# Zero-weight fillers, another gate for the last chunk's MLP weights, and a re-planned order in a fused attention and MLP block

## The chip, the core and the metric

The kernel runs on one core of one Trainium2 chip. The time is the device time of one execution in microseconds (us); what is compared is the median over runs. Five engines work side by side, each through its own instruction queue: TensorE (PE, matmuls; its weight loads are shown apart as PEld), VectorE (DVE), ScalarE (ACT), GpSimd (POOL) and SyncE (SP). Nearly all DMA transfers are issued by SP, one after the other.

## The reference, cut to what matters

```python
x = A_x                                   # 1 x 2048 x 640, bf16
mod = (silu(c) @ w_mod).reshape(1, 6, 1, 640)
sa, ca, ga, sb, cb, gb = mod[:, 0] ... mod[:, 5]
h = layernorm(x) * (1 + ca) + sa
q, k, v = split(h @ wqkv)                 # 32 heads of 20
p = softmax(q @ k.T * 20 ** -0.5)         # 2048 x 2048 for each head
x = x + ga * ((p @ v) @ wo)
h = layernorm(x) * (1 + cb) + sb
x = x + gb * (((h @ w_gate) * (h @ w_up)) @ w_down)   # 640 -> 1536 -> 640
```

The 32 score matrices of 2048 x 2048, their exponentials and their products with V are most of the work.

## The kernel before, in words

**Chunks and items.** The queries are cut into six chunks (L474): 512, 512, 256, 256, 256 and 256 of them. In each chunk there are eight items, each a set of four heads. An item walks over the 2048 keys in 16 key tiles of 128. In one group, PE multiplies four heads at a time by matmuls that each use 32 rows of the array (L1511, `ps_all<-QT,KT`), into a pair of PSUM banks. There are two such pairs for ACT, so that PE fills one while ACT works on the other.

**Exponentials.** Most groups go to ACT: one activation of 128 x 1024 (L1548) writes bf16 probabilities to `PP`. The rest is done by DVE with integer arithmetic on the bits of the number, in "D units": L1572 (scores to int16 bits, `DB`), L1604 and L1612 (two masks, `DSS`), and a product of the two by DVE (L1609) or POOL (L1624).

**Products with V.** `PP` or `DSS` times `Vf` (L2177) go into the running bank of the item: a PSUM bank in which each item sums over its key tiles, in four quadrants of 32 rows. `Vf` holds V of every head with a column of ones (for the sum of the softmax), and behind the last head a column block of zeros. The item's end is T1 (L1704), a reciprocal (L1709), the normalisation T3 (L1711, POOL) and T4 (L1720), and then four or five small DMAs on SP into `Ocp` (L1732).

**Suffix of a chunk.** Once a chunk's items are done, `suffix(ci)` does the output projection, the second layernorm, its transpose `h2T`, twelve rounds of gate and up (L961, `ps_all<-h2T,stg`), their product `hprod`, the down projection (L961, `ps_all<-wd,hprod`) and the output. For the chunks before the last, this work is spread between the scores of the next chunk. Its gate and up weights come in pairs of 160 KB each (L1917, SP) into a ring of three buffers, `stg`; a pair is asked for once its buffer is free. The last chunk's suffix has nothing to hide behind. Ten of its twelve pairs have buffers of their own, `stx`, and in the kernel before they may be asked for as soon as chunk 4's attention output has been written out.

**Start.** Q, K and V are computed from x in the first 270 us, just ahead of the items that need them. Q and K go through rows in DRAM: `q_rows` and `k_rows` are written and then loaded in another layout as `QT` (L1289) and `KT`. Unused rows of `q_rows` are zeroed by DMAs that each cover 512 tokens (L1441, `q_rows<-Ocp`, 393 KB).

**The planner.** Nothing in the loops above fixes the order of instructions. A planner in Python (`Sched`, driven by `pick_pe` and its helpers) runs before compilation: it steps through time with a cost for each task (constants such as `PE_SWITCH` for PE going from one kind of matmul to another, `PV_W` for a product pass, `HAM_*` and `FILL_*` for keeping PE busy) and writes out a fixed order for PE, ACT, DVE, POOL and SP. `emit_program` adds the semaphores. A task has a priority and a gate, which is the number of score groups before which it is not taken. `STAGE` overrides constants item by item. Its numbers shape the order; on the chip, each instruction simply starts when its engine comes to it and its semaphores are there.

**Fillers.** Where the planner thinks that PE would fall idle too long, `do_fill` puts in matmuls whose result nobody reads: identity times a broadcast identity, into a free general bank (L2510), four quadrants of 512 columns.

Of the kernel before, what the change touches and what calls it, by code (L numbers as in the profile page):

```python
# [12 lines left out]

SEM = 60.0
PE_DRAIN = 170.0
PE_SWITCH = 102.0
PE_BACK = 112.0
PV_W = 219.0
X_FIRST = 0.0
ACT_LAT = 250.0  # L20
DVE_LAT = 40.0
# [10 lines left out]
STEAL_END = 66197.894  # L32
STEAL_GAP = 200
HAM_W = 3413.3
HAM_MIN = 2550.0
LKTOL = 300.0


# [92 lines left out]
class Sched:  # L131
# [143 lines left out]
    def step_engine(self, eng):  # L275
        if self.free_at[eng] > self.t:
            return False
        self.pull(eng)
        rl = self.readyl[eng]
        for k, task in enumerate(rl):  # L280
            if task.dead:
                self.readyl[eng] = rl = [x for x in rl if not x.dead]
                return self.step_engine(eng)
            if task.gate > self.progress or (task.cond is not None and not task.cond()):
                continue
            if self.locked(eng, task):
                continue
            if self.acquire(task, self.t):
                rl.pop(k)
                self.lock(eng, task)  # L290
                self.finish_issue(task, self.t, task.dur)
                self.free_at[eng] = self.t + task.dur
                return True
        if eng == "act":
            return self.steal()
        return False
# [53 lines left out]
def emit_program(nc, sched, nsem_dma=56):  # L350
# [130 lines left out]
PV_KEEP = 2  # L481
# [10 lines left out]
EAGER = 7  # L492
# [3 lines left out]
XBACK = 0  # L496
HOLD = 110
PVTOL = 249
XDPRIO = 1.343
# [2 lines left out]
GU_ONE = 1  # L502
XCONT = 0
T3_POOL = 1
HEAD_OUT = 2
NPS = 4
TS_4X, TT_2X = 600.0, 1145.0
# [21 lines left out]
PREEMPT = 0.0  # L529
PRE_M = 0.3  # L530
PV0N = 1
GATE_F = (0.446, 0.6, 0.5, 0.5, 0.5, 1.0)
FILL_MIN = 4190.746
FILL_HARD = 3000.0
FILL_T0, FILL_TH, FILL_MINH = 2300.0, 17000.0, 7500.0
FILL_MODE = 'P'
DUP_MIN = 0.0
# [17 lines left out]
NTERM = 2  # L555

STAGE = {
    0: {"D_LATE": 16, "PVMIN": 2, "X_LATE": -179.96, "XDPRIO": 1.343, "LKTOL": 300.0, "FILL_MIN": 4190.746, "HOLD": 95, "TPRIO": 0.75, "PVTOL": 249, "EAGER": 9, "X_HALF": 0.0, "XBACK": 0, "D_RES": 74, "PVCAP": 12, "PVMAX": 14, "STEAL_GAP": 200, "PV_KEEP": 2},
    2: {"DL": 0.376},
    4: {"HOLD": 53.4},  # L560
    5: {"HOLD": 88.7, "STEAL_GAP": 176.5},
    7: {"DL": 0.501},
    9: {"LKTOL": 115.1},
    10: {"X_HALF": 5.8},
    11: {"DL": 0.443, "EAGER": 4, "FILL_MIN": 3731.3, "X_HALF": 38.6},
    12: {"DL": 0.459, "LKTOL": 438.4, "STEAL_GAP": 303.4, "EAGER": 10, "X_HALF": 21.8},
    13: {"DL": 0.417, "FILL_MIN": 4496.3, "STEAL_GAP": 266.2, "X_HALF": 20.9},
    15: {"LKTOL": 166.0, "PVMAX": 5, "EAGER": 10, "XBACK": 1},
    16: {"PVCAP": 10, "PVMAX": 3, "EAGER": 10, "FILL_MIN": 5086.4},
    17: {"X_HALF": -35.2},  # L570
    18: {"EAGER": 3, "X_LATE": -36.1, "HOLD": 42.4, "PVMIN": 1},
    19: {"DL": 0.471, "EAGER": 2, "X_HALF": 94.7},
    20: {"DL": 0.391},
    21: {"EAGER": 6, "FILL_MIN": 4510.3, "X_HALF": 24.2, "D_LATE": 5},
    22: {"PVMAX": 7, "X_HALF": 147.8, "EAGER": 9, "X_LATE": -21.9, "HOLD": 66.8},
    23: {"HOLD": 124.7, "X_HALF": 14.5},
    24: {"DL": 0.464},
    25: {"DL": 0.549, "PV_KEEP": 3, "X_LATE": 36.2},
    26: {"DL": 0.411, "X_LATE": 65.8, "PVMAX": 3, "EAGER": 8},
    27: {"DL": 0.473, "XBACK": 1, "HOLD": 186.0, "FILL_MIN": 3881.8, "X_LATE": -1.8},  # L580
    28: {"X_HALF": 33.6, "FILL_MIN": 4310.0, "XBACK": 0},
    29: {"PVMAX": 7, "X_LATE": -9.2},
    30: {"X_LATE": -109.9, "HOLD": 140.4, "XBACK": 1},
    31: {"X_LATE": 202.7, "D_RES": 21},
    32: {"PVCAP": 11, "X_HALF": -25.7, "X_LATE": 197.5},
    33: {"DL": 0.442},
    34: {"PVMIN": 5, "X_HALF": 27.8, "XBACK": 1},
    35: {"X_HALF": -31.6, "PVMAX": 14},
    36: {"DL": 0.524},
    37: {"X_LATE": -50.4},  # L590
    40: {"XBACK": 1, "HOLD": 36.3},
    41: {"X_LATE": 52.1, "X_HALF": -52.1},
    44: {"X_LATE": -66.5, "EAGER": 4, "D_RES": 10},
    47: {"FILL_MIN": 5302.0},
    48: {"PVCAP": 14, "FILL_MIN": 3192.3},
}
XHALF = 1
STG_G0, STG_G, XC_G = 12, -10, -20
# [12 lines left out]
def build_kernel(nc, A_x, A_wqkv, A_wo, B_x, B_w_gate, B_w_up, B_w_down, c, w_mod, out):  # L611
# [195 lines left out]
    def dve(dur, f, deps=(), prio=3.0, **k):  # L807
        return sc.add(Task("dve", dur, f, deps, prio=prio, **k))
# [770 lines left out]
    for qi, (it, us) in enumerate(dquads):  # L1579
# [36 lines left out]
        if X_POOL and qi % X_POOL == X_POOL - 1 and qi < len(dquads) - X_LAST and all(  # L1616
                dquads[z][0] == it for z in range(qi, min(len(dquads), qi + X_TAIL + 1))):
            st_["xby"] = None
            for x in range(X_PIECES):
                w = 2048 // X_PIECES  # L1620

                def fxp(e, x=x, w=w, st_=st_):
                    d = DSl[st_["ss"][0]][:, x * w:x * w + w].bitcast(BF16)
                    return e.tensor_tensor(d, DBl[st_["slot"]][:, x * w:x * w + w].bitcast(BF16), d, ALU.mult)  # L1624
                t = Task("pool", w * POOL_NS + 180.0, fxp, [tm, te], prio=2.0 + .1 * qi + .01 * x, name=f"XP.{qi}")
                t.lk = 2
                t.cond = lambda st_=st_: st_["xby"] != "dve"

                def on_p(task, x=x, st_=st_):
                    if x == 0:  # L1630
                        st_["xby"] = "pool"
                        st_["xd"].dead = True
                        sc.left -= 1
                    xjob[0] = X_PIECES - 1 - x
                    if x == X_PIECES - 1:
                        sB0.done(st_["slot"], task)
                        st_["src"][0] = [task]
                t.on_start = on_p
                sc.add(t)
                st_.setdefault("xps", []).append(t)  # L1640
            t = term(fx, [tm, te], TT_2X, "X", src=0, last=True)
            st_["xd"] = t
            t.prio = XDPRIO + .001 * qi
            c0, o0 = t.cond, t.on_start
            t.cond = lambda c0=c0, st_=st_: st_["xby"] is None and c0() and xjob[0] >= XBACK

            def on_x(task, o0=o0, st_=st_):
                o0(task)
                st_["xby"] = "dve"
                for x in st_["xps"]:  # L1650
                    x.dead = True
                sc.left -= X_PIECES
                sc.nx += 1
            t.on_start = on_x
        else:
            term(fx, [tm], TT_2X, "X", src=0, last=True)
# [37 lines left out]
    def item_end_tasks(it):  # L1694
        ci, j = items[it]
        if ci == NC - 1 and j == 0:
# [9 lines left out]
        t1.acq = [(sOT, "o", 1)]  # L1706
        t1.on_start = lambda task: G.done(item_info[it]["bank"], task)
        item_info[it]["t1"] = t1
        t2 = dve(155, lambda e: e.reciprocal(invT[:, 0:nb32].unsqueeze(2),  # L1709
                                            OT[:, 0:n].rearrange("p (b c) -> p b c", c=32)[:, :, 0:1]), [t1], prio=pe_)  # L1710
        f3 = lambda e: e.tensor_tensor(  # L1711
# [1 line left out]
            OT[:, 0:n].rearrange("p (b r c) -> p b r c", c=32, r=2),  # L1713
            invT[:, 0:nb32].rearrange("p (b r) -> p b r", r=2).unsqueeze(3).to_broadcast([128, nb32 // 2, 2, 32]), ALU.mult)
        direct = j == NSET - 1 and ci == NC - 1
        if T3_POOL and not direct and not (END3 and j == NSET - 1):
            t3 = pool(n * 2.2 + 200, f3, [t2], prio=0)
        else:
            t3 = dvl(sb_cost(n, 1.04), f3, [t2], prio=pe_)
# [39 lines left out]
    def suffix(ci):  # L1759
# [148 lines left out]
        for fc in range(FT):  # L1908
            use_x = tail and fc < nsx
            wbuf, dm = [], []  # L1910
            for w_, wv in enumerate((wgv, wuv)):
                cell = {}
                if use_x:
                    cell["t"] = stx[fc][:, w_, :, :]

                def f(e, wv=wv, fc=fc, cell=cell):
                    return e.dma_start(cell["t"], wv[:, :, fc * 128:(fc + 1) * 128])  # L1917
                t = dma("sp", int(STG_B * 128 * KD * 128 * 2), f,
                        (sfx_done["qdead"] if fc < nsq else first) + oc_ready[(NC - 2, CHUNKS[-2][1] // 128 - 1)] if use_x else
                        kp_use if ci == 0 else [], prio=16 + ci + .01 * fc,  # L1920
                        gate=int(gstart[NC] - 40) if tail and not use_x else 0 if tail else max(0, gb + (STG_G0 if ci == 0 else STG_G)))
                if not use_x:
                    t.acq = [(sStg[w_], "s", 1)]

                    def on0(task, cell=cell, w_=w_):
                        cell["i"] = task.slots["s"]
                        cell["t"] = stg[cell["i"]][:, w_, :, :]
                    t.on_start = on0
                wbuf.append(cell)
                dm.append(t)  # L1930
# [156 lines left out]
    def clk():  # L2087
        return 2.0 if sc.cold else 1.0
# [292 lines left out]
    def pick_pe(t):  # L2381
# [111 lines left out]
            return True  # L2493
        return t > FILL_T0 and fill_ok(t, fill_deps) and do_fill(t)

    def do_fill(t):
        mode = FILL_MODE if pvstate["sidx"] else "X"
        start = mode_start(mode, t)
        fs = G
# [86 lines left out]
```

## Time and profile before

| what | value |
|---|---|
| median of 3 runs | 806.67 us (805.83 to 808.27) |
| profiled execution: its time, its span | 806.1 us, 804.3 us |
| ACT exps, L1548 | 812, 1145 ns each, 746.8 us busy |
| scores, L1511 (PE) | 3136 matmuls, 319.1 us |
| products with V, L2177 (PE), from PP and DSS | 2504 and 1264 matmuls, 164.0 and 84.9 us |
| gate and up, L961 (PE) | 2272 matmuls, 122.3 us |
| down, L961 (PE) | 1384 matmuls, 63.2 us |
| D units, L1572 (DVE) | 424 tiles, 683 ns each, 283.6 us |
| fillers, L2510 (PE) | 108 matmuls, 27 passes |
| POOL's products, L1624 | 264, 1157 ns each, 300.1 us |
| first exp starts, last exp ends | 16.9 us, 775.85 us |

Busy times can overlap: weight loads run beside matmuls, and pipelined instructions have a duration longer than their spacing (an exp takes 1145 ns, and one begins about every 0.9 us). "Idle before, releaser" at the end of a row says how long the engine stood before such instructions and what ended most of that wait; in a timeline the same stands in brackets, with the releaser behind the arrow. A matmul's quoted time in the timeline is that of a run of matmuls, counted behind the x.

### The profile page before, as it was taken

Reading aid. Unit: us, or ns where it says so; the run is one execution under the profiler, and the core shown is the slowest. Engines: PE = TensorE matmul, PEld = TensorE weight load, DVE = VectorE, ACT = ScalarE, POOL = GpSimd, SP = SyncE. Lnnn points to the kernel's source line nnn. Section 1 sums busy time; section 2 is a strip of 40 time slices with the busy share of each in tenths; the row PEclk is TensorE's granted clock in tenths of the full one; section 3 lists DMA queues with packets and bytes.
Section 4 is the critical chain, followed back from the end, with each engine's and each line's share of the span. In section 5 each row is a group of like instructions: output and inputs, shape, how many; then the busy total and the mean of one; then the engine's idle time right before and its main releaser. Section 6 shows DMA issues by size and latency. Waiting matters only on the chain.

```text
span 804.3 us, 34189 instructions
## 1 busy us (share of the span) xinstructions
PE 786.4 (98%) x14875; PEld 345.9 (43%) x14875; DVE 688.5 (86%) x1355; ACT 762.8 (95%) x847; POOL 361.9 (45%) x373
## 2 busy tenths in 40 slices
PE   8999999999999999999999999999999999998998
PEld 4433423332233232323444444455555554544567
DVE  7989797898999899999877888988898989796654
ACT  6899899999999999999999999999999999998951
POOL 2443436545464643234664433654653434635400
PEclk9999999999999999999999999999999999999999
DMA  9843212202341522101301232100342054527400
GB/s 297 241 122 79 66 53 67 63 24 70 106 107 45 152 66 52 42 7 47 72 18 23 47 78 55 39 16 24 97 88 56 24 121 90 109 58 159 89 22 18
DMA packets 136387, 60.49 MB, mean 75 GB/s; under 512 B 100703, under 2 KB 136239, under 8 KB 136239
## 3 DMA queue, kind: packets, MB, share of 16 engines
q1 hardware_dynamic: 135311, 57.16, 28.0%
q8 instruction: 118, 1.93, 1.0%
q10 hardware_dynamic: 928, 1.15, 0.4%
q14 instruction: 30, 0.25, 0.1%
HBM read 46.70 MB, written 8.99 MB: 69 GB/s over the span
## 4 chain that ended last, share of the span: by engine, by line
PE 60%; ACT 24%; DVE 9%; issue 4%; DMA 2%; SPq 1%; ACTq 0%; DVEq 0%
ACT PP L1548 24%; PE ps_all L1511 20%; PE ps_all L961 18%; PE ps_all L2177 14%; DVE DB L1572 3%; PE ps_all L957 3%; PE ps_all L1221 2%; DMA wm<-in_w_mod_dram 1%; DVE DSS L1612 1%; DVE DSS L1604 1%; DVE DSS L1609 1%; SPq L1732 1%; PE ps_all L2510 1%; PE ps_all L1118 1%; PE ps_all L1157 1%
## 5 line engine op out<-in xcount | busy, mean ns | idle before, releaser
L1548 ACT ACTIVATE PP<-ps_all 128x1024 bf16<-128x1024 f32 x812 | 746.8, 1145 | 7.5 <-PE ps_all L1511 5.2
L1624 POOL TENSOR_TENSOR DSS<-DB,DSS 128x512 bf16<-128x512 bf16 x264 | 300.1, 1157 | 335.3 <-DVE DSS L1612 276.6
L1572 DVE TENSOR_SCALAR DB<-ps_all 128x512 int16<-128x512 f32 x424 | 283.6, 683 | 60.7 <-PE ps_all L1511 58.3
L1511 PE MATMUL ps_all<-QT,KT 32*128 32x256 bf16 (+2 forms) x3136 | 319.1, 307 | 7.0 <-ACT PP L1548 4.1
L1511 PEld LDWEIGHTS ps_all<-QT,KT 32*128 32x128 bf16 x3136 | 89.2, 92 | 229.2 <-ACT PP L1548 191.5
L2177 PE MATMUL ps_all<-PP,Vf 128*32 128x256 bf16 (+2 forms) x2504 | 164.0, 311 | 0.6 <-DVE Vf L1310 0.6
L961 PE MATMUL ps_all<-h2T,stg 128*32 128x256 bf16 (+2 forms) x2272 | 122.3, 303 | 0.8 <-DMA stg<-in_B_w_up_dram 0.5
L2177 PEld LDWEIGHTS ps_all<-PP,Vf 128*32 128x32 bf16 (+1 forms) x2504 | 50.2, 94 | 81.7 <-issue 74.7
L2177 PE MATMUL ps_all<-DSS,Vf 128*32 128x256 bf16 (+1 forms) x1264 | 84.9, 313 | 0.0
L1604 DVE TENSOR_SCALAR DSS<-DB 128x2048 int16<-128x2048 int16 x106 | 73.6, 695 | 0.6
L1612 DVE TENSOR_SCALAR DSS<-DB 128x2048 int16<-128x2048 int16 x106 | 73.1, 690 | 0.0
L961 PEld LDWEIGHTS ps_all<-h2T,stg 128*32 128x32 bf16 x2272 | 51.4, 96 | 30.2 <-issue 20.3
L961 PE MATMUL ps_all<-wd,hprod 128*32 128x320 bf16 (+1 forms) x1384 | 63.2, 279 | 0.0
L1711 POOL TENSOR_TENSOR OTn<-OT,invT 128x256 bf16<-128x256 f32 (+1 forms) x42 | 34.8, 829 | 34.2 <-DVE invT L1709 34.2
L1609 DVE TENSOR_TENSOR DSS<-DB,DSS 128x2048 bf16<-128x2048 bf16 x40 | 49.3, 1231 | 0.0
L2177 PEld LDWEIGHTS ps_all<-DSS,Vf 128*32 128x32 bf16 (+1 forms) x1264 | 31.3, 96 | 20.1 <-issue 8.5
L961 PEld LDWEIGHTS ps_all<-wd,hprod 128*32 128x32 bf16 x1384 | 31.0, 96 | 18.0 <-issue 12.2
L961 PE MATMUL ps_all<-wV,hT 128*32 128x160 bf16 x1280 | 37.6, 234 | 0.6 <-DVE DB L1572 0.2
L1221 PE MATMUL ps_all<-hT,wk 128*32 128x512 bf16 (+1 forms) x360 | 31.6, 382 | 0.4 <-DVE DB L1572 0.2
L1221 PE MATMUL ps_all<-hT,wq 128*32 128x512 bf16 x375 | 31.4, 382 | 0.0
L961 PEld LDWEIGHTS ps_all<-wV,hT 128*32 128x32 bf16 x1280 | 24.0, 96 | 15.4 <-issue 8.4
L961 PE MATMUL ps_all<-wo,Ocp 128*32 128x320 bf16 (+1 forms) x628 | 30.1, 287 | 0.0
(131 smaller groups left out, 525.5 us busy)
## 6 DMA issues: line engine op xcount, KB each, us to landing
stg<-in_B_w_gate_dram SPq DMA_DIRECT2D x62, 160.0 KB
stg<-in_B_w_up_dram SPq DMA_DIRECT2D x62, 160.0 KB
KT<-k_rows SPq DMA_DIRECT2D x112, 32.0 KB
wm<-in_w_mod_dram SPq DMA_DIRECT2D x3, 800.0 KB
x<-in_A_x_dram SPq DMA_DIRECT2D x7, 320.0 KB
k_rows<-KPA SPq DMA_DIRECT2D x16, 128.0 KB
QT<-q_rows SPq DMA_DIRECT2D x32, 64.0 KB
wd<-in_B_w_down_dram SPq DMA_DIRECT2D x1, 1920.0 KB
```

The lines of the kernel that those rows point to most:

```text
L957: return lambda e, b: e.matmul(ps[:, b, c0:c0 + n], lhs(), rhs(), start=st, stop=sp)
L961: return lambda e, b: e.matmul(ps[32 * x:32 * x + 32, b, c0 + o:c0 + o + w], lhs()[:, 32 * x:32 * x + 32], rhs() if w == n else rhs()[:, o ...
L1221: f = [lambda e, b_, k=k, x=x: e.matmul(ps[x:x + min(32, w - x), b_, :], wx[:, k, r0 + x:r0 + min(x + 32, w)], hT[tc][:, k, :], tile_posit ...
L1511: ems.append(lambda e, i=i, kt=kt: e.matmul(dstf()[:, i * u.n:(i + 1) * u.n], KT[32 * u.s:32 * u.s + 32, u.j, kt * 128:(kt + 1) * 128], QT ...
L1548: return e.activation(PPs[g % 2][:, cellp["p"], 0:nu * 512], ps[:, b0:b0 + nu, :].rearrange("p b c -> p (b c)"), AFT.Exp, scale=ESCALE)
L1572: return e.tensor_scalar(DBl[st_["slot"]][:, x * 512:(x + 1) * 512], bank(cell["b"]), EBIAS, 0.0, op0=ALU.add, op1=ALU.max)
L1604: return e.tensor_scalar(DSl[st_["ss"][0]][:, :], DBl[st_["slot"]][:, :], 0x7F, 0x3F00, op0=ALU.bitwise_and, op1=ALU.bitwise_or)
L1609: return e.tensor_tensor(d, DBl[st_["slot"]][:, :].bitcast(BF16), d, ALU.mult)
L1612: return e.tensor_scalar(DSl[st_["ss"][1]][:, :], DBl[st_["slot"]][:, :], 0x7F80, 2, op0=ALU.bitwise_and, op1=ALU.bitwise_or)
L1624: return e.tensor_tensor(d, DBl[st_["slot"]][:, x * w:x * w + w].bitcast(BF16), d, ALU.mult)
L1711: f3 = lambda e: e.tensor_tensor(OTn[:, 0:n].rearrange("p (b c r) -> p b r c", c=32, r=2), OT[:, 0:n].rearrange("p (b r c) -> p b r c", c= ...
L2177: ems.append(lambda e, i=i, kt=kt, stt=stt, stp=stp: e.matmul(ps[32 * s:32 * s + mc, bk, 0:u.n], Vf[:, (kt * H + 4 * u.j + s) * VW:(kt * H ...
```

## The change

1. **Zero-weight fillers** (`ZFILL`). A new function `zero_fill` is tried first in `do_fill`. It multiplies the zero block of `Vf` with a broadcast identity and adds the result to the running value bank of the item that is under way, so it needs no bank of its own. One pass is four matmuls of 512 columns, or eight of 256.
2. **Weights of the last chunk.** Their loads no longer depend on the output of chunk 4's attention; instead they have gates, three score groups apart from the first score group of the last chunk on. The planner counts 500 ns for an issue of any gate or up load, where it counted 400.
3. **Planning.** If the scores of an exp come late, the planner counts that exp longer (24 ns less 0.2 of the slack). The costs of a switch and of a product pass go up by 3 and 2 ns, `HAM_MIN` and `FILL_HARD` go up, the `GATE_F` shares go down, and `STAGE` has other values in most items. The order that the planner writes differs through all of this on every engine, with the same scores, exponentials and products: it has 15,101 matmuls where there were 14,877, among them 43 zero-weight passes and one filler of the old kind, and more of the rounds of `wo`, `wd` and `h2T` are issued in halves.

```diff
-PE_SWITCH = 102.0
+PE_SWITCH = 105.0
-PV_W = 219.0
+PV_W = 221.0
-HAM_MIN = 2550.0
+HAM_MIN = 3000.0
...
             if self.acquire(task, self.t):
                 rl.pop(k)
                 self.lock(eng, task)
+                if eng == "act" and task.name[:1] == "E":
+                    slack = min(self.t - d.done - SEM for d in task.deps if d.mode == "S")
+                    task.dur += max(0.0, LATE0 - LATE1 * slack)
                 self.finish_issue(task, self.t, task.dur)
...
+STX_G, W_ISSUE = 3, 500.0
+ZFILL = 1
+LATE0, LATE1 = 24.0, 0.2
...
-GATE_F = (0.446, 0.6, 0.5, 0.5, 0.5, 1.0)
+GATE_F = (0.446, 0.5, 0.4, 0.4, 0.4, 1.0)
-FILL_HARD = 3000.0
+FILL_HARD = 3500.0
...
 STAGE = {
...
-    4: {"HOLD": 53.4},
-    5: {"HOLD": 88.7, "STEAL_GAP": 176.5},
+    3: {"PVTOL": 81.1, "X_HALF": -56.2},
+    4: {"HOLD": 116.6},
+    5: {"PVMAX": 14, "PV_KEEP": 3},
...
                 t = dma("sp", int(STG_B * 128 * KD * 128 * 2), f,
-                        (sfx_done["qdead"] if fc < nsq else first) + oc_ready[(NC - 2, CHUNKS[-2][1] // 128 - 1)] if use_x else
-                        kp_use if ci == 0 else [], prio=16 + ci + .01 * fc,
-                        gate=int(gstart[NC] - 40) if tail and not use_x else 0 if tail else max(0, gb + (STG_G0 if ci == 0 else STG_G)))
+                        (sfx_done["qdead"] if fc < nsq else first) if use_x else
+                        kp_use if ci == 0 else [], prio=16 + ci + .01 * fc, dur=W_ISSUE,
+                        gate=int(gstart[NC] - 40) if tail and not use_x else int(gstart[NC - 1]) + 1 + STX_G * fc if tail else max(0, gb + (STG_G0 if ci == 0 else STG_G)))
...
+    def zero_fill(t):
+        it = st_pv["item"]
+        if it >= len(items) or pvstate["sidx"] == 0:
+            return False
+        info = item_info[it]
+        if info["bank"] is None or any(first_pv[(it, s)] or left_pv[(it, s)] <= 0 for s in range(4)):
+            return False
+        n = spans[it][1]
+        start = mode_start("P", t)
+        bk = info["bank"]
+        z0 = NT * H * VW
+        rhs = ident[:].unsqueeze(1).to_broadcast([128, n // 128, 128])
+        ems = [lambda e, x=x: e.matmul(
+            ps[32 * x:32 * x + 32, bk, 0:n].rearrange("p (a b) -> p a b", b=128), Vf[:, z0:z0 + 32], rhs,
+            tile_position=(0, 32 * x), start=False, stop=False, skip_group_check=True) for x in range(4)] * (512 // n)
+        task = Task("pe", 216.0, ems, [p_vz], ctr="pex", mode="P", name="zfill")
...
     def do_fill(t):
+        if ZFILL and zero_fill(t):
+            return True
         mode = FILL_MODE if pvstate["sidx"] else "X"
```

More of the change, by code (lines that the diff above doesn't have):

```diff
@@ L557 @@
 STAGE = {
-    0: {"D_LATE": 16, "PVMIN": 2, "X_LATE": -179.96, "XDPRIO": 1.343, "LKTOL": 300.0, "FILL_MIN": 4190.746, "HOLD": 95, "TPRIO": 0.75, "PVTOL": 249, "EAGER": 9, "X_HALF": 0.0, "XBACK": 0, "D_RES": 74, "PVCAP": 12, "PVMAX": 14, "STEAL_GAP": 200, "PV_KEEP": 2},
+    0: {"D_RES": 74, "HOLD": 95, "X_LATE": -179.96, "XDPRIO": 1.343, "PVMIN": 2, "PV_KEEP": 2, "PVMAX": 14, "EAGER": 9, "FILL_MIN": 4270.2, "D_LATE": 16, "XBACK": 1, "PVTOL": 249, "TPRIO": 0.75, "X_HALF": 0.0, "PVCAP": 12, "STEAL_GAP": 200, "LKTOL": 300.0},
@@ L559 @@
+    1: {"PVTOL": 336.9, "PV_KEEP": 3},
     2: {"DL": 0.376},
-    4: {"HOLD": 53.4},
-    5: {"HOLD": 88.7, "STEAL_GAP": 176.5},
+    3: {"PVTOL": 81.1, "X_HALF": -56.2},
+    4: {"HOLD": 116.6},
+    5: {"PVMAX": 14, "PV_KEEP": 3},
+    6: {"PVTOL": 125.6},
     7: {"DL": 0.501},
[L563 to L572, printed above, removed]
-    20: {"DL": 0.391},
-    21: {"EAGER": 6, "FILL_MIN": 4510.3, "X_HALF": 24.2, "D_LATE": 5},
-    22: {"PVMAX": 7, "X_HALF": 147.8, "EAGER": 9, "X_LATE": -21.9, "HOLD": 66.8},
-    23: {"HOLD": 124.7, "X_HALF": 14.5},
@@ L577 @@
[L577 to L585, printed above, removed]
+    8: {"EAGER": 10},
@@ new lines @@
+    11: {"DL": 0.443, "LKTOL": 763.5, "X_LATE": 43.5, "D_RES": 16},
+    12: {"DL": 0.459},
+    13: {"DL": 0.417, "XBACK": 2, "PV_KEEP": 2, "PVMIN": 2},
+    14: {"EAGER": 11, "PVMAX": 6, "X_LATE": -77.4, "X_HALF": 66.3, "PVMIN": 1},
+    15: {"X_HALF": 80.7, "X_LATE": -106.1},
+    18: {"EAGER": 3, "PVTOL": 60.6, "PVMIN": 3, "FILL_MIN": 5815.1, "PVMAX": 15},
+    19: {"DL": 0.471, "EAGER": 6},
+    20: {"DL": 0.391},
+    21: {"X_HALF": 75.5, "EAGER": 5, "HOLD": 54.6, "PV_KEEP": 3},
+    22: {"PVTOL": 239.2, "X_LATE": 39.3},
@@ L586 @@
+    23: {"X_LATE": 39.3, "EAGER": 8},
+    24: {"DL": 0.464, "PV_KEEP": 2, "HOLD": 148.9, "EAGER": 6, "X_HALF": 26.1},
+    25: {"DL": 0.549},
+    26: {"DL": 0.411},
+    27: {"DL": 0.473, "D_RES": 67, "HOLD": 128.1, "X_HALF": -63.3},
+    28: {"EAGER": 3, "X_LATE": -17.8},
+    29: {"X_LATE": -42.2, "X_HALF": 22.7},
+    30: {"HOLD": 77.4, "D_LATE": 17, "X_HALF": -15.6},
+    31: {"PVMIN": 2, "HOLD": 175.3},
     33: {"DL": 0.442},
-    34: {"PVMIN": 5, "X_HALF": 27.8, "XBACK": 1},
-    35: {"X_HALF": -31.6, "PVMAX": 14},
+    34: {"PVTOL": 108.7, "X_LATE": 183.6},
@@ L589 @@
     36: {"DL": 0.524},
[L590 to L595, printed above, removed]
+    39: {"D_RES": 9, "PVMAX": 3},
+    40: {"X_HALF": 40.2, "PV_KEEP": 4, "XBACK": 1},
+    41: {"X_HALF": 136.5, "EAGER": 9},
+    42: {"PVTOL": 242.4, "X_HALF": -43.9},
+    43: {"X_LATE": -101.8},
+    44: {"PVCAP": 12, "PVMAX": 15},
+    45: {"PVCAP": 14, "EAGER": 5, "D_LATE": 15, "D_RES": 9, "X_LATE": -54.7, "LKTOL": 268.8},
@@ L596 @@
+    46: {"X_LATE": -38.9, "PV_KEEP": 1},
 }
@@ L1627, in build_kernel, with on_p @@
                 t.cond = lambda st_=st_: st_["xby"] != "dve"
-                def on_p(task, x=x, st_=st_):
+                def on_p(task, x=x, st_=st_, qi=qi, it=it, te=te):
                     if x == 0:
@@ L1645, in build_kernel, with on_x @@
             t.cond = lambda c0=c0, st_=st_: st_["xby"] is None and c0() and xjob[0] >= XBACK
-            def on_x(task, o0=o0, st_=st_):
+            def on_x(task, o0=o0, st_=st_, qi=qi, it=it, te=te):
                 o0(task)
@@ L1708, in item_end_tasks @@
         item_info[it]["t1"] = t1
+        pooled = T3_POOL and not (j == NSET - 1 and ci == NC - 1) and not (END3 and j == NSET - 1)
         t2 = dve(155, lambda e: e.reciprocal(invT[:, 0:nb32].unsqueeze(2),
@@ L1715, in item_end_tasks @@
         direct = j == NSET - 1 and ci == NC - 1
-        if T3_POOL and not direct and not (END3 and j == NSET - 1):
+        if pooled:
             t3 = pool(n * 2.2 + 200, f3, [t2], prio=0)
@@ L2494, in pick_pe @@
         return t > FILL_T0 and fill_ok(t, fill_deps) and do_fill(t)
+    def zero_fill(t):
[14 more added lines that the diff above has]
+        task = Task("pe", 216.0, ems, [p_vz], ctr="pex", mode="P", name="zfill")
+        sc.activity(start, 512.0)
+        task.seq = 0
+        sc.left += 1
+        sc.finish_issue(task, start, 216.0 * clk())
+        sc.pe_mode = "P"
+        sc.pe_end = start + 216.0 * clk()
+        sc.free_at["pe"] = sc.pe_end
+        sc.nzero += 1
+        return True
     def do_fill(t):
+        if ZFILL and zero_fill(t):
+            return True
         mode = FILL_MODE if pvstate["sidx"] else "X"
```

## Prediction

> **What bounds the kernel now.** I read the busy line first, then the chain that ended last, then the exp (L1548) in windows, then the timeline where its windows fall short.
>
> ```profile
> PE 786.4 (98%) x14875; PEld 345.9 (43%) x14875; DVE 688.5 (86%) x1355; ACT 762.8 (95%) x847; POOL 361.9 (45%) x373
> PE 60%; ACT 24%; DVE 9%; issue 4%; DMA 2%; SPq 1%; ACTq 0%; DVEq 0%
> L1548 ACT ACTIVATE PP<-ps_all 128x1024 bf16<-128x1024 f32 x812 | 746.8, 1145 | 7.5 <-PE ps_all L1511 5.2
> ```
>
> PE (98%) and ACT (95%) are both nearly full, and the chain passes between them: PE cannot write the next scores until an exp frees a bank pair, and the exp cannot start without them. Who has the slack is read by stage, from the exp alone (ACT busy, count, granted clock, DMA share, GB/s):
>
> ```profile
> core 0: us, ACT busy (x), PEclk, DMA share, GB/s
> 100.00:200.00 100.00, 100.00 (x110) 1.00 0.21 55
> 520.00:620.00 100.00, 100.00 (x111) 1.00 0.24 57
> 668.00:718.00 50.00, 49.55 (x55) 1.00 0.38 82
> 718.00:768.00 50.00, 46.53 (x51) 0.97 0.53 112
> ```
>
> In the middle ACT is busy all the time, 110 or 111 exps in 100 us, so 0.90 to 0.91 us each. There ACT is the bound and PE's fillers and small delays cost nothing. Time is lost where ACT falls short: 3.47 us of the last window (50.00 - 46.53; 51 exps where 55 would fit), some at the start, and the tail after the last exp (ends 775.85; 28.4 us of PE work). The loss in the last window has one place:
>
> ```profile
> 726.53 0.56 SPq L1917 DMA_DIRECT2D stg<-in_B_w_up_dram  x1
> ...
> 728.99 0.29 PE L961 MATMUL ps_all<-h2Tt,stg 128*32 128x256 bf16 x4
> ...
> 731.42 0.46 PE L961 MATMUL ps_all<-h2Tt,stg 128*32 128x256 bf16 x12 [2.14 <-DVE DSS L1612]
> ...
> 732.25 1.02 ACT L1548 ACTIVATE PP<-ps_all 128x1024 bf16<-128x1024 f32 x1 [2.07 <-PE ps_all L1511]
> ```
>
> PE stands 2.14 us at a gate/up round of chunk 4. The named releaser (L1612) writes DSS, which this matmul does not read; the round reads stg, whose up half was issued at 726.53 and landed at 731.33 by its semaphore record, just before PE went on. Ahead of it in SP's queue stood four loads for the last chunk (stx, issued 723.68 to 725.38, 0.53 each). ACT then waits 2.07. The clock falls as well:
>
> ```profile
> core 0: us, PE busy (x) PEld busy (x) DVE busy (x) ACT busy (x) POOL busy (x), PEclk, DMA share, GB/s
> 730.00:732.00 2.00, 0.58 (x16) 0.37 (x16) 1.35 (x3) 0.17 (x1) 0.57 (x1) 1.00 0.86 196
> 732.00:734.00 2.00, 2.00 (x42) 1.18 (x42) 0.23 (x1) 1.30 (x2) 2.00 (x3) 0.59 1.14 228
> 734.00:736.00 2.00, 2.00 (x40) 0.91 (x28) 0.79 (x2) 1.49 (x2) 1.93 (x2) 0.56 0.06 14
> ```
>
> The trace has 3.41 us at half clock (732.36 to 735.77) and three further ACT waits in it: 0.45, 0.51, 0.20. Wait and slow clock together are the four lost exps: 4 x 0.905 = 3.6 us.
>
> The Trainium skill ("TensorE: Matmul & The Clock Gate", "What's actually happening") has the clock halved after at least one idle window of about 3.4 us. Here a 2.1 us wait sufficed, so row and rule differ. By the rule the stall would be worth only its 2.07 us; the sum goes by the 3.6 of the windows.
>
> **Part 1, weights of the last chunk.** Their gate moves from 0 with a dependency on chunk 4's attention output to three score groups apart from chunk 5's first score on, and the planner counts 500 ns an issue. In the written order, 10 of these loads now go out between chunk 3's own pairs, and two instead of four stand directly ahead of chunk 4's pair 5. Counting from xckc's issue, T0 (714.98 before), and giving each issue ahead its row time: pair 5's up half goes out at T0+8.8, up to T0+12.3 if SP has slow issues as before (1.55, 1.38 and 2.03 instead of 0.53). It lands 2.7 (unloaded rows of stg) to 4.8 us (loaded) later: T0+11.5 to T0+17.1. Its round stands 18 score groups after T0, 18 x 0.905 = 16.3; it had 16. So this stall goes: -3.6. What is late next is pair 6: issue T0+15.9 to +19.4, landing +18.6 to +24.2, needed after 23 groups, +20.8. Wait 0 to 3.4; I take 0.6, near the lower end, since most of the landing range is before the need. +0.6.
>
> **Part 2, fillers.** 27 four-product passes on identity in a bank of their own become 43 zero-weight passes and one old one: 17 more. No row shows a zero-weight product; the nearest, L1221's four-quadrant passes, runs 20 matmuls (5 passes) in 1.08 us, so 0.216 a pass. With the switches (some 20 more into and out of product mode) the cost is between 0 and 17 x 0.216 = 3.7. Most new ones lie in score groups 191 to 264, where ACT is busy 100.00 of 100 and PE would otherwise wait: 0. If PE had no slack there it would be the 3.7. No bank is taken any more, so a filler cannot hold up a gate/up round; the trace shows no such hold-up, so no gain is taken.
>
> **Part 3, the order.** The planner's changed constants act on the chip only through the order it writes. By row prices all PE work grows from 759.0 to 764.7 us (+5.7: 3.7 fillers, the rest rounds issued in halves). From chunk 4's scores to the end it is 209.8 against 209.6, level. After the last score it is 26.0 against 27.8: 48 more matmuls wd,hprodt of 32x320 at 1.54/40 us = 1.85, eight products fewer. As the work ahead of the last score shrinks by as much, I take 0 of bounds 0 to +1.85.
>
> One q_rows zero write (L1441) moves from behind to ahead of a QT load that PE waits for:
>
> ```profile
> 88.77 0.92 SPq L1289 DMA_DIRECT2D QT<-q_rows  x2
> ...
> 90.54 0.48 SPq L1441 DMA_DIRECT2D q_rows<-Ocp  x1
> ...
> 90.93 0.40 PE L1511 MATMUL ps_all<-QT,KT 32*128 32x512 bf16 x4 [0.64 <-DMA QT<-q_rows]
> 94.96 3.77 ACT L1548 ACTIVATE PP<-ps_all 128x1024 bf16<-128x1024 f32 x4 [1.34 <-PE ps_all L2177]
> ```
>
> Moved past: three q_rows writes, four Ocp, the QT load. Ahead of the load it costs its own issue, 0.5, and up to 4.95, which is what an earlier such write (issued 78.08) took to land. Loads behind that one took 3.2 to 4.6 against 1.8. PE is the bound there already (ACT lost 0.25 + 0.54 + 1.34 around it), so it counts: +0.9, nearest to its issue.
>
> Reserve: the planner now lengthens an exp whose scores come late (24 ns less 0.2 of the slack), which should bring scores forward. What it could win is bounded: 812 exps cost 0.905 at best and 0.9175 on the mean in the middle, 10 us in all; in this order the places with over 1.0 us of PE work between two scores go only from 75 to 73, their excess in chunk 0 grows 7.8 to 9.8, and those of the last chunk fall from 10 to 5. Bounds -3 to +2; I take -0.5.
>
> **Sum** against the profiled execution, 806.1 (span 804.3, 1.8 around it): -3.6 + 0.6 + 0 + 0 + 0.9 - 0.5 = -2.6, so 803.5. That execution is 0.6 below the median 806.67 and inside the runs shown, so the median should go to **804.1**. Its own range, from the uncertain terms, is 801.5 to 806.5.
>
> **Rivals.**
> *The stall moves.* Pair 6, or 5 again, comes over 2 us late, the clock halves again, and the whole 3.6 returns. For: pair 6's landing range reaches 3.4 past its need, and slow issues are in the trace. Against: two groups more room for pair 5. 804.1 - 0.6 + 3.6 = 807.1.
> *PE sets the rate.* It is 98% busy and 60% of the chain; wherever its work per exp passes 0.905 us, added passes and switches push the scores back and no cover hides them. It decides in score groups 191 to 441, once the slack there is under 0.216 for a pass. All 5.7 then count: 804.1 + 5.7 = 809.8. For: PE rows leave 2% idle, and the planner's reserve is not in PE's count. Against: ACT 100.00 of 100 at 100 to 200 us.
> *The reserve works.* A third of the 10 us that exps lose comes back, by scores waiting ready: 804.1 - 3.3 = 800.8. For: ACT loses small pieces everywhere. Against: the level count of long places.
> *The loads do not move.* Dependencies still hold the last chunk's loads behind xckc from the sixth pair on, so SP's queue is as full as before: 807.1 as in the first, counted with it.
>
> **Chances.** Forecast 0.45, stall moves 0.18, PE sets the rate 0.20, reserve works 0.17. A measurement of this kernel can tell about 0.3%, 2.4 us (its runs lie 805.83 to 808.27). The forecast lies just over that bound, so 0.28 of its 0.45 is faster, 0.15 within, 0.02 slower; the reserve is faster; of the moved stall 0.01 is faster, 0.14 within, 0.03 slower; PE's rate is slower with 0.19 of its 0.20. Together faster 0.46, within 0.30, slower 0.24. The range that leaves out no more than 2 in 10 is 800.4 to 809.4.
>
> **What would show it.** The stall: no PE wait over 1 us between 715 and 740, granted clock 1.00 throughout, 54 or 55 exps in the window that had 51. Pair 6: a wait at the next gate/up round under 1 us. Fillers: 43 passes of Vf on ident at some 0.22 us, ACT still full in 190 to 262. QT: the wait near 90 grows from 0.64 to about 1.5. Tail: last exp to end 28.4, at most 30.3. Wrong would be exps of over 0.92 us on the mean in the middle (PE's rate), or a new clock drop after 715.

## The result, and the profile after

The change made the kernel slower: 814.3 us (median of 6 runs, 811.46 to 816.61) against 806.25 before (6 runs, 803.75 to 808.27), a ratio of 1.0101 with a 95% interval of 1.0074 to 1.0128. A repetition beside other experiments gave 812.05 us and 1.0083 (1.0055 to 1.0111). The profiled execution took 814.25 us, with a span of 812.4.

The page of the changed kernel, the rows that answer to those shown of before (line numbers are 7 to 8 higher):

```profile
PE 793.0 (98%) x15099; PEld 350.7 (43%) x15099; DVE 694.0 (85%) x1353; ACT 765.8 (94%) x848; POOL 365.7 (45%) x377
PE 70%; ACT 16%; DVE 7%; DMA 3%; issue 3%; SPq 1%; ACTq 0%
L1555 ACT ACTIVATE PP<-ps_all 128x1024 bf16<-128x1024 f32 x812 | 749.4, 1096 | 10.7 <-PE ps_all L1518 8.2
```

The busy shares hardly move, but the chain does: PE had 60% of it and has 70%, ACT had 24% and has 16%. ACT's idle time before its exps grew from 7.5 to 10.7 us. By stage, for the exp alone (ACT busy, count, granted clock, DMA share, GB/s):

```profile
core 0: us, ACT busy (x), PEclk, DMA share, GB/s
100.00:200.00 100.00, 98.08 (x108) 1.00 0.20 55
520.00:620.00 100.00, 99.21 (x109) 1.00 0.21 51
668.00:718.00 50.00, 50.00 (x56) 1.00 0.44 96
718.00:768.00 50.00, 45.26 (x50) 0.93 0.55 117
```

The two middle windows, which were full, are full no longer, and the last one, which should have gained four exps, lost one more. The timeline there:

```profile
734.69 2.29 SPq L1925 DMA_DIRECT2D stx<-in_B_w_up_dram  x1
...
737.03 3.92 SPq L1740 DMA_DIRECT2D Ocp<-OcT  x5
...
741.52 0.53 SPq L1925 DMA_DIRECT2D stg<-in_B_w_up_dram  x1
...
744.58 0.72 PE L968 MATMUL ps_all<-h2Tt,stg 128*32 128x256 bf16 x12 [3.20 <-DMA stg<-in_B_w_up_dram]
...
745.88 1.02 ACT L1555 ACTIVATE PP<-ps_all 128x1024 bf16<-128x1024 f32 x1 [3.46 <-PE ps_all L1518]
```

This is pair 6 of chunk 4's weights. Pair 5 came in time (issued 732.27, landed 736.00 by its semaphore record). Behind it in SP's queue stand four more loads of the last chunk, the last of which held the queue for 2.29 us, and then five Ocp writes of 3.92 us in all. Pair 6 is issued at 741.52 and lands at 744.53. PE waits 3.20 us and the clock halves (busy times of the engines, granted clock, DMA share, GB/s in windows of 2 us):

```profile
core 0: us, PE busy (x) PEld busy (x) DVE busy (x) ACT busy (x) POOL busy (x), PEclk, DMA share, GB/s
742.00:744.00 2.00, 0.00 (x0) 0.00 (x0) 1.97 (x5) 0.41 (x1) 0.00 (x0) 0.71 0.91 206
744.00:746.00 2.00, 1.42 (x24) 0.66 (x28) 0.89 (x1) 0.12 (x1) 0.00 (x0) 0.50 1.29 231
746.00:748.00 2.00, 2.00 (x40) 1.03 (x36) 0.00 (x0) 1.51 (x2) 0.00 (x0) 0.50 0.45 78
748.00:750.00 2.00, 2.00 (x37) 0.72 (x26) 0.21 (x1) 1.40 (x2) 0.00 (x0) 0.59 0.03 6
```

From the clock column, (0.29 + 0.50 + 0.50 + 0.41) x 2 us / 0.5 = 6.8 us at half clock, twice the 3.41 of before. ACT waits 3.46, 0.49, 0.60 and 0.19: 4.7 us, where it lost 3.2 before. The pair's buffer was not what held it back: in a run below in which this pair goes to the front of the queue (`a_sp`), it is issued 10.9 us after xckc, the load that the prediction counts from, and here 18.4 us after it.

To see where the rest went I worked out, from the starts of the exps in each trace, by how much the intervals between them exceed 0.900 us, in stretches of exps (us):

| stretch | before | changed | difference |
|---|---|---|---|
| start of the first exp | 16.9 | 16.4 | -0.6 |
| exps 0 to 100 | 9.9 | 13.1 | +3.2 |
| exps 100 to 300 | 3.2 | 4.8 | +1.6 |
| exps 300 to 700 | 7.8 | 10.0 | +2.2 |
| exps 700 to 811 (the stall) | 7.0 | 7.1 | +0.1 |
| tail after the last exp | 28.5 | 30.0 | +1.5 |
| span | 804.3 | 812.4 | +8.1 |

Of the 3.2 in the first row of exps, some 2.5 are a clock that halved from about 22.6 us on in this execution (3.4 us by its clock column), after PE had waited 0.99 us for layernorm data. In the profile of the repetition it did not happen, and that row reads 10.6.

### The profile page after: what moved, and what is told of

It reads as the page before. It is cut to its first block, busy times and chain, and to the rows that moved or that the text cites. A ratio compares the mean times of both kernels' runs of the same rounds, so it can differ in the third digit from the quotient of the medians.

```text
span 812.4 us, 34617 instructions
## 1 busy us (share of the span) xinstructions
PE 793.0 (98%) x15099; PEld 350.7 (43%) x15099; DVE 694.0 (85%) x1353; ACT 765.8 (94%) x848; POOL 365.7 (45%) x377
## 3 DMA queue, kind: packets, MB, share of 16 engines
q8 instruction: 120, 1.97, 1.0%
q10 hardware_dynamic: 928, 1.15, 0.4%
## 4 chain that ended last, share of the span: by engine, by line
PE 70%; ACT 16%; DVE 7%; DMA 3%; issue 3%; SPq 1%; ACTq 0%
PE ps_all L1518 24%; PE ps_all L968 21%; PE ps_all L2185 17%; ACT PP L1555 16%; PE ps_all L1228 3%; PE ps_all L964 3%; DVE DB L1579 2%; DMA x<-in_A_x_dram 2%; SPq L1740 1%; DMA stg<-in_B_w_up_dram 1%; DVE DSS L1619 1%; DVE DSS L1611 1%; PE ps_all L2516 1%; DVE DSS L1616 1%; PE ps_all L1125 1%
## 5 line engine op out<-in xcount | busy, mean ns | idle before, releaser
L1555 ACT ACTIVATE PP<-ps_all 128x1024 bf16<-128x1024 f32 x812 | 749.4, 1096 | 10.7 <-PE ps_all L1518 8.2
L1631 POOL TENSOR_TENSOR DSS<-DB,DSS 128x512 bf16<-128x512 bf16 x268 | 304.8, 1158 | 316.5 <-DVE DSS L1619 278.8
L2185 PEld LDWEIGHTS ps_all<-PP,Vf 128*32 128x32 bf16 x2504 | 49.4, 94 | 81.7 <-issue 75.4
L1611 DVE TENSOR_SCALAR DSS<-DB 128x2048 int16<-128x2048 int16 x106 | 75.5, 712 | 0.4
L1619 DVE TENSOR_SCALAR DSS<-DB 128x2048 int16<-128x2048 int16 x106 | 74.8, 706 | 0.4 <-PE ps_all L2185 0.4
L968 PEld LDWEIGHTS ps_all<-wd,hprod 128*32 128x32 bf16 x1420 | 32.7, 96 | 16.3 <-issue 10.1
L1711 DVE STREAM_TRANSPOSE OT<-ps_all 128x256 f32<-128x256 f32 (+2 forms) x49 | 25.6, 523 | 10.7 <-PE ps_all L2185 10.6
```

Source lines behind the costliest of these rows:

```text
L968: return lambda e, b: e.matmul(ps[32 * x:32 * x + 32, b, c0 + o:c0 + o + w], lhs()[:, 32 * x:32 * x + 32], rhs() if w == n else rhs()[:, o ...
L1555: return e.activation(PPs[g % 2][:, cellp["p"], 0:nu * 512], ps[:, b0:b0 + nu, :].rearrange("p b c -> p (b c)"), AFT.Exp, scale=ESCALE)
L1611: return e.tensor_scalar(DSl[st_["ss"][0]][:, :], DBl[st_["slot"]][:, :], 0x7F, 0x3F00, op0=ALU.bitwise_and, op1=ALU.bitwise_or)
L1619: return e.tensor_scalar(DSl[st_["ss"][1]][:, :], DBl[st_["slot"]][:, :], 0x7F80, 2, op0=ALU.bitwise_and, op1=ALU.bitwise_or)
L1711: t1 = Task("dve", n * 1.1 + 70, lambda e: e.transpose(OT[:, 0:n], ps[:, item_info[it]["bank"], 0:n].rearrange("p (b q r) -> p b r q", q=3 ...
L2185: ems.append(lambda e, i=i, kt=kt, stt=stt, stp=stp: e.matmul(ps[32 * s:32 * s + mc, bk, 0:u.n], Vf[:, (kt * H + 4 * u.j + s) * VW:(kt * H ...
```

## The experiments

A difficulty comes first: the planner rewrites the whole order when one number changes. So there are two kinds of experiments. Some keep the written order and edit it just before it is emitted; each aims at one cause. The others are planned anew.

**Order kept: pair 6 ahead of the queue.** The same edit in both kernels, on SP's list alone:

```diff
+    pair6 = [al[k] for k in nm("W4.5")]            # chunk 4, sixth pair
+    last = al[nm("W4.7")[-1]]
+    stx_l = [t for t in al[nm("W4.3")[-1]:nm("W4.7")[-1]] if t.name[:3] == "W5."]
+    free = max((d for t in pair6 for d in t.deps), key=al.index)
+    al = [t for t in al if t not in stx_l and t not in pair6]
+    k = al.index(free) + 1
+    al[k:k] = pair6
+    k = al.index(last) + 1
+    al[k:k] = stx_l
     nw = emit_program(nc, sc)
```

In the changed kernel:

> The changed kernel, every instruction the same but SP's order: pair 6 of chunk 4's weights goes out as soon as its buffer is free, ahead of the five Ocp writes, and the six loads of the last chunk that stood between pairs 4 and 6 go behind pair 8. Theory 'the stall moved to pair 6': ACT's waits there (3.46 + 0.49 + 0.60 + 0.19 = 4.7 us) go, the clock does not fall near 742, 814.3 - 4.7 = 809.6; about 1.5 of the change's 8 us is this stall's excess over the one of before (3.2). Rival 'PE sets the rate': PE is behind anyway, what is saved here is waited for at the next scores, 812 or more.

Measured (`a_sp`): 813.28 us, ratio to before 1.0092 (1.006 to 1.0124). In the kernel before:

> The kernel before, with the same edit of SP's order alone (pair 6 as soon as its buffer is free, the seven loads of the last chunk between pairs 4 and 6 behind pair 8). Stall theory: ACT's waits of 2.07 + 0.45 + 0.51 + 0.20 = 3.2 us go and nothing else changes: 806.3 - 3.2 = 803.1. Rival 'a transfer is late next': pair 8 or 9 stalls behind the seven loads and the time stays at 806.

Measured: 805.58 us, 0.9991 (0.9968 to 1.0015). Both numbers of the stall theory (809.6 and 803.1) missed, and those of the rivals (812 or more, and 806) came. For the kernel before the rival was that a transfer is late next; for the changed one it was PE's rate, but there too the timeline shows a late transfer. First the changed kernel with the edit, then the kernel before with it:

```profile
751.01 0.34 PE L968 MATMUL ps_all<-h2Tt,stg 128*32 128x256 bf16 x4 [3.35 <-DMA stg<-in_B_w_up_dram]
```

```profile
743.85 0.46 PE L961 MATMUL ps_all<-h2Tt,stg 128*32 128x256 bf16 x12 [2.18 <-DMA stg<-in_B_w_up_dram]
```

The wait is as long as it was and only stands later. The loads that were pushed back now hold up a later pair. So what is wrong is not the place of pair 6 alone: the queue has too much in it between 715 and 760 for either of these orders. Whether SP's issuing or the transfers themselves are the limit is not separated, as each later edit takes both out of the stretch. In the changed kernel the up half of pair 6 landed 3.01 us after its issue, so it was issued late. In the kernel before, that of pair 5 took 4.80 us (726.53 to 731.33), where others issued in an emptier stretch took 2.7 to 2.9; there the slow landing is about the whole wait of 2.14.

**Order kept: the last chunk's ten late loads behind everything.** They are needed from about 785 us on, and after the last Ocp write SP has nothing to do:

```diff
+    moved = [t for t in al if t.name in ("W5.5x", "W5.6x", "W5.7x", "W5.8x", "W5.9x")]
+    al = [t for t in al if t not in moved]
+    k = max(k for k, t in enumerate(al) if t.name == "Ocp") + 1
+    al[k:k] = moved
     nw = emit_program(nc, sc)
```

> The kernel before, same order but for ten SP instructions: the loads of the last chunk's pairs 6 to 10 go behind the last Ocp write, so that none of them stands between chunk 4's pairs. They are then issued near 765 to 772 and needed from 785 on. Queue theory (the stall is SP's queue being full between 715 and 760, and moving seven loads within that stretch only moved the wait to 742): ACT's 3.2 us go, clock 1.00 there, 806.4 - 3.2 = 803.2. Rival 'the loads come late in the tail instead': the gate/up rounds after the last exp wait, tail over 28.5 us, 806 or more.

Measured, in the kernel before: 801.52 us, 0.9965 (0.9947 to 0.9982), the queue theory's number less 1.7. The exps in the window of the stall:

```profile
core 0: us, ACT busy (x), PEclk, DMA share, GB/s
718.00:768.00 50.00, 49.56 (x55) 1.00 0.42 94
```

55 exps where there were 51, at full clock, and the tail is 28.5 us as before.

> The changed kernel with the same edit. Queue theory: the wait of 3.4 us and what follows at half clock go, 814.3 - 4.7 = 809.6; what is then left over the kernel before with the same edit (6 us) is order, not weights. Rival: the tail waits, 814 or more.

Measured, in the changed kernel: 806.08 us, 1.0015 (0.9999 to 1.0031), 3.5 us under the 809.6 of the queue theory. Its window (the profiled execution, 808.69 us, is one of the two longest of twelve):

```profile
core 0: us, ACT busy (x), PEclk, DMA share, GB/s
718.00:768.00 50.00, 50.00 (x56) 1.00 0.38 89
```

Taking the ratios to before, the queue's wait costs the changed kernel 0.0068 (1.0083 of the repetition less 1.0015), 5.5 us, and the kernel before 0.0035, 2.8 us. With the wait gone from both, the new order is still slower by 1.0015 - 0.9965 = 0.0050, some 4 us. With the intervals of the ratios these three are 2.9 to 8.1, 1.4 to 4.3 and 2.1 to 5.9 us. With the first measurement's 1.0101 in place of 1.0083 the 5.5 would be 6.9. The repetition was run to settle how much of the distance the wait is:

> The changed kernel again, unaltered, beside the others: how often does the clock fall in it, and is its distance to itself without the queue's wait (806.1) the 4.7 us of ACT's waits that one profile shows, or 8? Theory 'one long wait brings two windows at half clock': 811.5 to 816, granted clock 0.992 to 0.998 over the span (0.004 is 6.5 us at half clock), none at 1.0.

Measured: 812.05 us, granted clock 0.994 to 0.998, none at 1.0, as expected. In its profile ACT waits 3.07, 0.40 and 0.60 at the stall, 4.1 in all. The 5.5 lies nearer to that than to 8, but its interval holds both, so this is not settled. Of the theory's mechanism the profile shows half: PE waits 3.28 us, and one stretch of 3.41 us at half clock follows, not two.

**Order kept: the new fillers issue nothing.**

```diff
         task = Task("pe", 216.0, ems, [p_vz], ctr="pex", mode="P", name="zfill")
+        task.emits = []
```

> The changed kernel, same order, but the 43 zero-weight passes issue nothing (no part of the result is lost). Theory 'ACT hides them': at most 1 us either way, unless the clock falls for want of them: each drop would cost 1 to 3 us, 815 to 818. Rival 'PE sets the rate': 43 passes of 0.216 us are 9.3 us of PE work; those that stand where exps come late cost their length, 809 to 812, and the late exps between exp 100 and 700 fall from 261 towards the 194 of before.

Measured: 822.25 us, 1.0189 (1.0149 to 1.0229), granted clock 0.973 to 0.987. Both theories asked for less. The 43 passes cost nothing that shows, and they are worth 7 to 9 us (0.0088 of the ratio against the full change, 0.0106 against its repetition). The profile puts the loss where the clock falls: in the row of exps 300 to 700 it has 19.2 us where the full change has 10.0, and in that stretch the clock is at half for 6.8 us from 405.6 on, for 17.1 from 429.5 on and for 3.4 from 668.4 on. One of the places where passes stood, in the kernel without them:

```profile
core 0: us, PE busy (x) PEld busy (x) DVE busy (x) ACT busy (x) POOL busy (x), PEclk, DMA share, GB/s
402.00:404.00 2.00, 1.30 (x24) 0.49 (x24) 2.00 (x5) 2.00 (x4) 0.43 (x1) 1.00 0.07 19
404.00:406.00 2.00, 1.30 (x26) 0.37 (x18) 2.00 (x2) 2.00 (x4) 0.84 (x2) 0.89 0.22 70
406.00:408.00 2.00, 1.82 (x26) 0.76 (x28) 0.43 (x1) 1.96 (x3) 1.03 (x1) 0.50 0.14 42
```

ACT is full (2.00 of 2.00) and PE has time to spare (1.30). Without the passes the clock halves at the end of this, and then PE is what ACT waits for. The late exps of the middle did not go away: between exps 450 and 600 there are 92 intervals of 915 ns or more without the passes, 91 with them, and 57 in the kernel before. So the fillers are not what makes exps late there; the rest of the order is.

**Planned anew: the parts.** Four kernels take one or two parts of the change each. Fillers alone (`ZFILL = 1` in the kernel before):

> The kernel before with the zero-weight fillers alone; the planner then writes another order with the same costs and item table. Theory 'an order that the item table was not searched for is worse, whatever the edit': 810 to 823, with late exps spread over the span and a longer tail. Theory 'fillers are good or neutral': 803 to 807.

Measured: 816.29 us, 1.014 (1.0121 to 1.0159), as the first theory asked. The tail is 33.8 us, 5.3 longer than before, and ACT waits 2.54 at a pair of weights. The new weights gate and issue cost alone:

> The kernel before with the new gate and issue cost of the last chunk's weights alone, re-planned. Theory 'the weights part moves the stall': a wait of 2 to 3.5 us at one of chunk 4's pairs, 806 to 809. Theory 'it removes it': no such wait, 803. Theory 'any re-planning is worse': 810 or more.

Measured: 804.35 us, 0.9989 (0.9972 to 1.0006). In its profile ACT has no wait over 0.2 us left between 640 and 765, and the granted clock is 1.0 in 10 of 12 runs: alone, this part does what it says. A tail of 29.7 us (28.5 before) and one new ACT wait of 0.63 at 636 take most of the gain back. The same ten loads stand behind xckc here (714.12 to 726.13), all ahead of the five Ocp writes at 733.82, and no pair is waited for. So a full queue does not bring the wait in every order. Fillers and weights together, with the planning constants and the item table of before:

> The kernel before with the new fillers and the new gate for the last chunk's weights, but with the planning constants and the item table of before and no lengthened exps. Theory 'the re-planned order is the loss': 804 to 808, as before, give or take a stall at chunk 4's weights. Rival 'fillers or weights are the loss': 811 to 815, as the full change.

Measured: 823.11 us, 1.0197 (1.0159 to 1.0236), tail 36.2 us. Neither theory asked for so much. The two planning costs alone, which no instruction on the chip contains:

```diff
-PE_SWITCH = 102.0
+PE_SWITCH = 105.0
...
-PV_W = 219.0
+PV_W = 221.0
```

> The kernel before with the change's two planning costs alone (a switch 105, a product pass 221 ns), re-planned with its old item table. Neither number reaches the chip but through the order. Theory 'an order that the table was not searched for is worse': 812 to 825. Theory 'truer costs give a better order': 806 or less.

Measured: 828.29 us, 1.0284 (1.0256 to 1.0312), the slowest of all and above both theories. And the full change with the old fillers:

> The changed kernel planned with the old fillers, all else as changed. Theory 'the table fits one set of costs and fillers only': 815 to 826, worse than the full change. Theory 'the new fillers are the loss': 806 to 810.

Measured: 824.74 us, 1.0221 (1.0189 to 1.0254), as the first theory asked. Of these five only the weights part stays level. By the traces its PE order is that of before up to some 333 us, where that of the fillers alone leaves it near 65 us and that of the costs alone near 54. The item table gives the 814 of the full change with the fillers, weights and costs that it came with, and 825 with the old fillers. That a table fits only what it came with explains all this, but it is not shown: none of the parts was run with a table made for it.

**A version that beats both.** With the ten loads moved, the largest wait left was near 90 us. One more move on SP:

```diff
+    two = [t for t in sc.all if t.name == "QT"][1:3]
+    free = max((d for t in two for d in t.deps), key=sc.all.index)
+    sc.all = [t for t in sc.all if t not in two]
+    k = [k for k, t in enumerate(sc.all) if t.name == "Ocp" and k > sc.all.index(free)][1] + 1
+    sc.all[k:k] = two
```

> The kernel before with the last chunk's ten late loads behind the last Ocp write (801.5) and one more move on SP: the two QT loads that scores wait for near 90 us go ahead of the third of four Ocp writes, and are issued when the q_rows writes have landed (86.6) instead of 88.4. Queue theory: ACT's 0.25 + 0.38 + 1.34 = 2.0 us there shrink by up to 1.8, 799.7 to 801. Rival 'the Ocp writes or PE are late next': 801.5.

Measured: 800.87 us, 0.9944 (0.9924 to 0.9964), the best of all, where the change has 1.0101. But PE no longer waits for QT here, and ACT still loses 0.25 and 1.23 at the place: PE has 48 matmuls of the V projection (1.15 us) between two scores. The move itself made 0.65 us by the medians (801.52 - 800.87), and the intervals overlap, so its worth is not shown.

## Why the prediction was wrong

It forecast 804.1 us and named four other ways; 814.3 lies outside its range. Both of its signs of being wrong came: the clock fell after 715, and from exp 100 to exp 700 an exp began every 0.925 us on the mean (0.918 before), over the 0.92 that it gave as the sign of PE's rate. Step by step:

- **The stall.** The first half was right: two groups more room were enough for pair 5, which landed in time. The second half failed, at "Wait 0 to 3.4; I take 0.6". Pair 6's up half went out at T0 + 18.95 (741.52 - 722.57) and landed at T0 + 21.96, both inside the ranges given. But PE came to it at T0 + 18.8, not 20.8, so it waited 3.20. This is the rival "the stall moves", and it was priced as the old stall, 3.6. The rival "the loads do not move" holds too. Part 1 took it as new that ten of the last chunk's loads go out early. But by the traces ten of the twenty are issued ahead of xckc in both kernels (684.09 to 690.94 before, 681.01 to 695.72 changed) and ten behind it, so behind xckc the queue had as many of them as before. With the wait came two stretches at half clock in one profile and one in another, and taking the queue's wait away gave 5.5 us by the ratios. I had looked for the place where a pair is late next and not at the sum of what SP has to issue. Moving the loads of one pair within the stretch moved the wait in both kernels, and taking the ten loads out of it ended the wait in both. The sum is not all: with the weights part alone the same ten loads are behind xckc and no wait came.
- **Fillers at nothing.** Right in cost: between exps 450 and 600 the late exps stayed (92 and 91) when they were taken out, and so did the 0.97 wait at 102 us (below). The rival "PE sets the rate" is refuted as far as the passes go; that scores come late in the middle did happen, by the rest of the order (next point). Its 809.8, the nearest of the times named, is in part luck: the passes in it cost nothing, and the stall that stayed is not in it. The term missed a size on the other side: what the passes hold up is the clock, 7 to 9 us of it.
- **"Reserve -0.5".** The term had the wrong sign. The exps from 100 to 700 lost 3.8 us more, where 0.5 less was forecast. The count of places with over 1.0 us of PE work between two scores was level and did not see it: 69 more intervals were 915 ns or longer (336 against 267), most of them by 20 to 60 ns, and a few places are worse. One of them:

```profile
100.56 0.95 PE L968 MATMUL ps_all<-wV,hT 128*32 128x160 bf16 x32
...
102.24 0.39 PE L1518 MATMUL ps_all<-QT,KT 32*128 32x512 bf16 x2
...
102.99 1.02 ACT L1555 ACTIVATE PP<-ps_all 128x1024 bf16<-128x1024 f32 x1 [0.97 <-PE ps_all L2185]
```

  The V projection stands between scores in this order, and the exp waits. The same wait is in all five executions of this order that were profiled (0.97 to 0.98 at the same exp), the one without fillers among them, and there is none at this exp before. Which of the planning constants made it was not separated, since any of them rewrites the order.
- **Tail at 0 of 0 to 1.85.** It measured +1.5, in all five profiles of this order alike (30.0 against 28.5). After the last exp, first before, then changed:

```profile
L961 PE MATMUL ps_all<-wd,hprodt 128*32 128x320 bf16 x48 | 2.2, 302 | 0.0
```

```profile
L968 PE MATMUL ps_all<-wd,hprodt 128*32 128x320 bf16 x96 | 3.8, 300 | 0.0
```

  The count of 48 more matmuls was right and their price nearly (1.6, where 1.85 was forecast). What failed was the cover: "the work ahead of the last score shrinks by as much" pays nothing back where ACT, not PE, sets the time ahead of it. In the changed kernel ACT was busy for 24.00 of the 24 us from 758 to 782.
- **QT +0.9.** It measured about 0: PE waited 0.67 us for QT against 0.64. The load had to wait for q_rows anyway, and the zero write went out while it did.

Between the forecast of -2.6 and the profile's +8.1 lie 10.7 us: the stall that stayed (3.1, in the row of exps 700 to 811), the middle (4.3), the tail (1.5) and the start (1.7, where the clock fell in that one execution).

## What to carry to other kernels

When one transfer in a full queue is late, add up all that the queue must issue and carry in that stretch, and move work out of the stretch if you can; here putting one pair first only moved the wait to a later one, though one other order of the same loads had none. A planned order can hang on any single number in it: here two planning costs, changed by 3 and 2 ns, made the kernel 2.8% slower, so edit the written order for a test and do not plan anew. And work that moves behind the last instruction of the bounding engine counts in full, whatever it left behind.

## What was not expected of the hardware

The granted clock fell without a long wait. In the kernel without fillers PE's longest single idle time between 400 and 406 us was 0.52 us and it was busy for 1.30 of each 2.00 us in two windows; the clock was at half from about 405.6 on. The stretches at half clock are 3.41 us or a multiple of it: 3.41 after the wait of 2.14 us in the kernel before, 6.83 after the 3.20 in the changed one, and 6.83 and 17.07 without fillers. The Trainium skill ("TensorE: Matmul & The Clock Gate", "What's actually happening") gives a free-running window of 3.413 us, and the lengths agree with it. Its condition for the fall, one idle window, does not agree if idle means without matmuls, since a window of PE two thirds busy was enough here.

The length of a wait did not set the number of stretches: 3.20 us gave two in the changed kernel, but 3.28 us gave one in its repetition, 3.35 us gave one with pair 6 ahead of the queue, and 3.31 us gave three in the kernel without fillers. What differs between the first two is how the wait lies to windows of 3.41 us counted from the start of a stretch. In the changed kernel it spans two of them, in which PE was busy for 1.97 us (739.41 to 742.82) and 1.66 us (to 746.24), and each is followed by one at half clock. In the repetition nearly all of it lies in one (739.03 to 742.44, PE busy 0.84 us), and one follows. This is a reading of two traces, not a test.

Passes with zero weights, whose products are all zero, seem to have kept the clock up in the same place: it reads 1.00 from 396 to 410 us in the changed kernel, where 40 of their matmuls stand between 404.9 and 408.7, and PE was busy for 1.89 and 2.00 of 2.00 us in the windows from 404 and 406.
